# wq loaded in eight transfers of every eighth lane, the first ahead of w_out; x in two halves; w_out at a multiple of 512 bytes

## The chip, the cores and the metric

The kernel runs on one core of one Trainium2 chip. The metric is the time of one execution on the device, in microseconds (us); of several runs the median is given. The core's engines are named as in the profile: PE (TensorE), PEld (its weight loads), DVE (VectorE), ACT (ScalarE), POOL (GpSimd), SP (SyncE, which here only issues transfers). Transfers run on the core's 16 DMA engines. A *lane* is one of the 128 partitions of the on-chip memory.

## The reference

One decode step for four sequences: a layer norm of x, then attention over a cache of 4,096 keys and a gated MLP (gMLP) side by side, both added to x. All inputs are bfloat16.

```python
# x (4,1,640); k_cache, v_cache (4,32,4096,128); wq (640,4096); wo (4096,640)
# w_in (640,1728); w_sp (1,1); b_sp (1,); w_out (864,640)
xn = _layernorm(x)
q = (xn @ wq) as (4, 32 heads, 1, 128)
p = softmax(q . k_cache * 128**-0.5);  A = (p . v_cache) as (4,1,4096) @ wo
z = gelu(xn @ w_in);  z1, z2 = halves of z (864 each);  z2 = _layernorm(z2)
g = w_sp * z2 + b_sp;  B = (z1 * g) @ w_out
return x + A + B
```

The two caches are 134 MB each; wq is 5.2 MB, wo 5.2 MB, w_in 2.2 MB, w_out 1.1 MB.

## The kernel before

The attention is cut into NT = 16 tiles: eight heads (HT) of one sequence each. A tile of k or of v is 8.4 MB, [128 lanes, 256 rows of 128 numbers], and fills a slot of 64 KB in each lane: lane p holds 256 consecutive keys of one head. There are two slots for k (`k_slot`) and one for v (`v_slot`). The weights use the same slots before and after the caches: wq stands in a k slot at the start, w_in and w_out together in the v slot (`w_sb`), and wo in the v slot at the end. The last v tile goes to a k slot (`v_last`).

All large loads are issued by SP in the order of the program: w_out's first 768 rows (L109), wq (L114), w_in (L121), the other 96 rows of w_out in four transfers of four lanes each, lanes l, l+4, l+8, l+12 (L123), then k's tile 0 (L139). k's tile 1 follows when wq's slot is free, v's tile 0 (L145) when `w_sb` is, and from then on k and v alternate. ACT issues x (L104) and the two scalars w_sp and b_sp (L118, L119). Each issue carries a completion semaphore; there are eight of these for transfers, and they are used again and again.

wq has 640 rows of 4,096; lane p holds rows 5p to 5p+4, 40,960 bytes that are contiguous in both memories. w_in lies the same way (17,280 bytes a lane). w_out follows it in the lane, from byte 17,280: six rows of 1,280 bytes, 7,680 bytes a lane. x is four rows of 1,280 bytes in four lanes.

The work at the start: DVE makes the layer norm of x (L183 to L191), PE turns it (L203) into `xnT_r`, then q = xn wq is made in 40 matmuls (L271), turned into `qT` (L282), and `stage_q` spreads one sequence's q over the lanes (`qbc`, L435 and L443). `gmlp` follows on PE, DVE and ACT, reading w_in (L317) and at its end w_out (L216).

Then for each tile, in two halves: DVE multiplies the k tile by q in place (`product`, L449), adds its halves (`fold`, L463), PE sums by eights through an identity (`sums`, L475), DVE sums the rest (`row_sums`, L486); the maximum goes across the lanes (L495 to L524), ACT makes the exponentials (L542), DVE the mask by heads (L553), and PE the product with v (`weighted`, L568). After the last v tile, the output projection with wo (`group_proj`) ends the kernel. The order on PE, DVE, ACT and SP is the one written out in the loop; SP's loads wait where a slot is still being read.

Of the kernel before, what the change touches and what calls it, by code (L numbers as in the profile page):

```python
# [17 lines left out]
def kernel(  # L18
# [14 lines left out]
    nc = tc.nc  # L33
    P = nc.NUM_PARTITIONS
    Bsz, Sq, D = A_x.shape
    _, H, S, Dh = A_k_cache.shape
    HD = A_wq.shape[1]
    F = B_w_in.shape[1]
    Fh = F // 2
    DC = D // P  # L40
# [30 lines left out]
    NFC = NFF + TK  # L71
# [22 lines left out]
    def k_slot(name):  # L94
        return kp.tile([P, SLOT], BF16, tag="k", name=name)

    def v_slot(name):
        return vp.tile([P, SLOT], BF16, tag="v", name=name)
# [2 lines left out]
    start_t = pmp.tile([P, 4 * 512], BF16, tag="pm", name="start_t")  # L101
    x_bf = start_t[:Bsz, 0:D]
    xn_bf = start_t[:Bsz, D : 2 * D]
    nc.scalar.dma_start(out=x_bf, in_=A_x.flatten_outer_dims())  # L104

    w_sb = v_slot("w_sb")
    w_in_sb = w_sb[:, 0 : DC * F].rearrange("p (c n) -> p c n", c=DC)
    w_out_sb = w_sb[:, DC * F : DC * F + NFC * D].rearrange("p (k n) -> p k n", k=NFC)
    nc.sync.dma_start(  # L109
        out=w_out_sb[:, 0:NFF, :], in_=B_w_out[0 : NFF * P].rearrange("(p k) n -> p k n", k=NFF)  # L110
    )

    wq_t = k_slot("wq")[:, 0 : DC * HD].rearrange("p (c n) -> p c n", n=HD)
    nc.sync.dma_start(out=wq_t, in_=A_wq.rearrange("(p c) n -> p c n", c=DC))  # L114

    wsp_bf = const.tile([1, 1], BF16)
    bsp_bf = const.tile([1, 1], BF16)
# [4 lines left out]
    for l in range(TL // TE):  # L122
        nc.sync.dma_start(  # L123
            out=w_out_sb[:TL, NFF:NFC, :].rearrange("(e l) k n -> e l (k n)", e=TE)[:, l],
            in_=B_w_out[F0:Fh].rearrange("(e l k) n -> e l (k n)", e=TE, k=TK)[:, l],
# [56 lines left out]
    for i in range(NSTAT):  # L182
# [5 lines left out]
        out=rstd[:], in_=mv[:, 1:2], func=ACT.Sqrt, bias=eps_tile[:Bsz], scale=1.0  # L188
# [3 lines left out]
        out=xn_bf,  # L192
# [9 lines left out]
    for c in range(DC):  # L202
        nc.tensor.transpose(  # L203
            out=xnT_ps[:, c, :], in_=xn_v[:, c, :], identity=ident[:Bsz, :Bsz]
# [3 lines left out]
        out=xnT_r[:], in_=xnT_ps[:, :, :, None].to_broadcast([P, DC, Bsz, REP])  # L208
# [5 lines left out]
    def add_out(lhsT, rhs, start=False, stop=False):  # L214
# [14 lines left out]
        out=own[:], in_=ident_f[:].rearrange("p (h l) -> p h l", h=HT), axis=AX.X, op=ALU.add  # L229
# [4 lines left out]
        out=pick[:, :, GW - HT : GW],  # L234
        in_=ident_f[:].rearrange("p (j h c) -> p c h j", c=CB, h=HT),
# [5 lines left out]
        out=row_head_f[:],  # L241
        in_=ident_f[:WR, :WR].rearrange("p (g b h) -> p g h b", g=NG, h=HT),
# [5 lines left out]
        out=row_head[:],  # L248
        in_=row_head_f[:].rearrange("p g h -> p (g h)")[:, :, None].to_broadcast([WR, WH, WL]),
# [3 lines left out]
        out=row_batch_f[:],  # L253
        in_=ident_f[:WR, :WR].rearrange("p (g b h) -> p b g h", g=NG, h=HT),
# [12 lines left out]
    for t in range(2):  # L267
        for c in range(DC):
            for j in range(CG):
                n = CG * t + j  # L270
                nc.tensor.matmul(  # L271
                    out=q_ps[t][GW * j : GW * (j + 1), :],
# [6 lines left out]
    for t in range(2):  # L279
        qT_ps = ps_m.tile([P, HQ, CG, Bsz, REP], BF16, tag="m", name="qT_ps")  # L280
        for n in range(HQ):
            nc.tensor.transpose(  # L282
                out=qT_ps[:, n].rearrange("p j b r -> p (j b r)"),
                in_=q_rows[:, t, n * Dh : (n + 1) * Dh],
# [3 lines left out]
            out=qT[:, CG * HQ * t : CG * HQ * (t + 1), :].rearrange(  # L288
                "p (j n) b -> p n j b", n=HQ
            ),  # L290
            in_=qT_ps[:, :, :, :, 0],
# [382 lines left out]
    with tc.manual_schedule(engines={E.PE, E.DVE, E.Activation, E.SP}):  # L674
# [62 lines left out]
        for h, (_, queue) in enumerate(halves):  # L737
            cols = slice(D // 2 * h, D // 2 * (h + 1))
# [31 lines left out]
```

## Time and profile before

| | |
|---|---|
| median of 3 runs | 661.44 us (661.08 to 661.54) |
| the profiled execution: its time | 661.22 us |
| its span, first to last instruction | 659.4 us |
| mean granted TensorE clock | 0.713 |
| DVE busy | 492.3 us (75%) |
| PE busy, PEld busy | 298.0 us (45%), 129.0 us (20%) |
| ACT busy, POOL busy | 34.7 us (5%), 2.1 us (0%) |
| read from the chip's main memory | 282.24 MB, 428 GB/s over the span |

A row of the timeline gives the start in us from the span's start, the busy time in us, the engine, the line of the kernel, the operation, the tiles (out<-in) and how many were merged; in brackets stands the engine's idle time before it and what ended that. SPq and ACTq are the rows of the issuing queues: the time there is that of the issue, not of the transfer. A row by stretches gives from:to, then each engine's busy time with the number of instructions, the granted clock, the mean busy share of the 16 DMA engines, and GB/s. A row of waits gives the engine and line, what it waited for, the us in total, the number of times, and the longest.

### The profile page before, as it was taken

How to read it: one execution, taken by the hardware profiler on the slowest of the kernel's cores; microseconds unless marked ns; L12 is line 12 of the kernel's file. 1: busy time of each engine (PE TensorE's matmuls, PEld its weight loads, DVE VectorE, ACT ScalarE, POOL GpSimd, SP SyncE). 2: the span in 40 equal slices, each digit the busy share in tenths (PEclk: the TensorE clock that was granted, in tenths of full speed). 3: DMA queues.
4: the chain of work that ended last, by engine and by line, in shares of the span. 5: the costliest groups of instructions: out<-in, count | busy, mean ns of one | idle time of the engine just before them, and what ended most of it. 6: DMA issues, size and time to landing. Idle time of an engine off the chain costs nothing.

```text
span 659.4 us, 4721 instructions
## 1 busy us (share of the span) xinstructions
PE 298.0 (45%) x2099; PEld 129.0 (20%) x2099; DVE 492.3 (75%) x224; ACT 34.7 (5%) x95; POOL 2.1 (0%) x15
## 2 busy tenths in 40 slices
PE   0513464535426253542626344362734616273656
PEld 0301121212112021210202112120311202121223
DVE  1249999959597795959879569986959699695861
ACT  0300000000000000000000000000000000000000
POOL 1000000000000000000000000000000000000000
PEclk9756676876858687585868757786685758668698
DMA  9999999999999999999999999999999999999996
GB/s 378 445 441 445 406 442 438 426 445 426 429 441 430 429 442 426 441 426 421 445 437 434 441 422 425 445 430 437 434 430 433 446 417 434 429 445 438 437 399 296
DMA packets 5696, 282.55 MB, mean 429 GB/s; under 512 B 656, under 2 KB 796, under 8 KB 1068
## 3 DMA queue, kind: packets, MB, share of 16 engines
q1 hardware_dynamic: 5656, 282.24, 99.0%
q8 instruction: 16, 0.26, 0.1%
q14 instruction: 4, 0.03, 0.0%
q10 hardware_dynamic: 20, 0.01, 0.0%
HBM read 282.24 MB, written 0.01 MB: 428 GB/s over the span
## 4 chain that ended last, share of the span: by engine, by line
DMA 49%; DVE 40%; PE 8%; issue 2%; ACT 1%; SPq 0%; DVEq 0%
DMA k_nat<-in_A_k_cache_dram 42%; DVE k_nat L449 24%; DVE k_nat L463 12%; DMA v_last<-in_A_v_cache_dram 6%; PE s_ps L475 6%; DVE s_sb L486 3%; PE pv L568 1%; ACT p L542 1%; DMA w_sb<-in_B_w_out_dram 1%; DVE m L495 1%; PE mT L500 0%; DVE nm L505 0%; PE out_ps L216 0%; DVE wide L628 0%; PE o_ps L591 0%
## 5 line engine op out<-in xcount | busy, mean ns | idle before, releaser
L449 DVE TENSOR_TENSOR k_nat<-k_nat,qbc 128x16384 bf16<-128x16384 bf16 x32 | 278.0, 8688 | 96.3 <-DMA k_nat<-in_A_k_cache_dram 96.3
L475 PE MATMUL s_ps<-k_nat,ident 128*128 128x512 bf16 x528 | 186.7, 532 | 137.7 <-DVE k_nat L463 137.7
L463 DVE TENSOR_TENSOR k_nat<-k_nat 128x8192 bf16<-128x8192 bf16 x31 | 136.7, 4410 | 0.0
L475 PEld LDWEIGHTS <-ident 128*128 128x128 bf16 x528 | 65.9, 130 | 248.0 <-DVE k_nat L463 121.6
L500 PE MATMUL mT<-ident_f,m 128*1 128x128 f32 x16 | 5.9, 366 | 157.9 <-DVE m L495 157.9
L568 PE MATMUL pv<-v_nat,pm 128*32 128x512 bf16 x960 | 56.2, 388 | 0.8 <-DVE pm L553 0.8
L486 DVE TENSOR_REDUCE s_sb<-s_ps 128x128 f32<-128x1024 f32 x32 | 39.0, 1218 | 3.8 <-PE s_ps L475 3.7
L568 PEld LDWEIGHTS <-pm 128*32 128x32 bf16 x1024 | 27.5, 101 | 36.1 <-issue 10.8
L500 PEld LDWEIGHTS mT<-ident_f,m 128*1 128x1 f32 x16 | 1.3, 79 | 165.7 <-DVE m L495 154.5
L553 DVE TENSOR_TENSOR pm<-p,own_c 128x2048 bf16<-128x2048 bf16 x16 | 19.6, 1226 | 15.7 <-ACT p L542 15.7
L542 ACT ACTIVATE p<-s_sb,nb 128x256 bf16<-128x256 f32 x16 | 8.1, 508 | 388.5 <-DVE nb_h L524 388.5
L591 PE MATMUL o_ps<-e,pick 128*32 128x128 f32 x128 | 17.0, 276 | 11.2 <-ACT e L578 11.2
L591 PEld LDWEIGHTS o_ps<-e,pick 128*32 128x32 f32 x128 | 12.7, 109 | 18.7 <-ACT e L578 18.7
L578 ACT COPY e<-pv 128x512 f32<-128x512 f32 x16 | 9.4, 586 | 70.9 <-PE pv L568 61.3
L287 DVE COPY qT<-qT_ps 128x64 bf16<-128x64 bf16 x2 | 0.4, 224 | 15.5 <-PE qT_ps L282 15.5
L516 PE MATMUL nb_ps<-nm,ones_row 1*128 1x8 f32 x32 | 9.2, 359 | 6.0 <-DVE nm L505 6.0
L505 DVE TENSOR_REDUCE nm<-mT 1x8 f32<-1x128 f32 x16 | 4.5, 279 | 7.5 <-PE mT L500 7.5
L516 PEld LDWEIGHTS nb_ps<-nm,ones_row 1*128 1x128 f32 x32 | 7.7, 299 | 10.6 <-DVE nm L505 9.9
L271 PE MATMUL q_ps<-wq,xnT_r 128*32 128x512 bf16 x40 | 4.2, 603 | 11.2 <-DMA wq<-in_A_wq_dram 11.2
L443 ACT CAST qbc<-qbc_ps 128x128 bf16<-128x128 f32 x16 | 4.3, 267 | 94.6 <-PE qbc_ps L435 94.6
L568 PE MATMUL pv<-v_last,pm 128*32 128x512 bf16 x64 | 6.3, 577 | 4.1 <-DMA v_last<-in_A_v_cache_dram 4.1
L608 PE MATMUL den<-ones_col,acc_h 128*32 128x1 f32 x8 | 1.0, 194 | 15.5 <-DVE acc_h L601 15.5
(93 smaller groups left out, 72.6 us busy)
## 6 DMA issues: line engine op xcount, KB each, us to landing
wq<-in_A_wq_dram SPq DMA_DIRECT2D x1, 5120.0 KB, 16.3
wo<-in_A_wo_dram SPq DMA_DIRECT2D x1, 2560.0 KB
w_sb<-in_B_w_in_dram SPq DMA_DIRECT2D x1, 2160.0 KB, 21.0
wo<-in_A_wo_dram SPq DMA_DIRECT2D x1, 1760.0 KB
w_sb<-in_B_w_out_dram SPq DMA_DIRECT2D x1, 960.0 KB
wo<-in_A_wo_dram SPq DMA_DIRECT2D x1, 640.0 KB, 24.6
k_nat<-in_A_k_cache_dram SPq DMA_DIRECT2D x16, 39.2
v_nat<-in_A_v_cache_dram SPq DMA_DIRECT2D x15, 33.3
```

The costliest lines, as they stand in the source:

```text
L449: nc.vector.tensor_tensor(out=part(i, u), in0=part(i, u), in1=qbcs[i][:, None, :].to_broadcast([P, UC, Dh]), op=ALU.mult,)
L463: nc.vector.tensor_tensor(out=t[:, :, 0:HD2], in0=t[:, :, 0:HD2], in1=t[:, :, HD2:Dh], op=ALU.add)
L475: nc.tensor.matmul(out=sums_ps[i][:, c : c + SC], lhsT=ident[:], rhs=t[:, c : c + SC, g * RW : (g + 1) * RW], start=(g == 0), stop=(g == n ...
L486: nc.vector.tensor_reduce(out=scores[i][:, u * UC : (u + 1) * UC], in_=sums_ps[i][:], axis=AX.X, op=ALU.add,)
L495: nc.vector.tensor_reduce(out=m1[:], in_=scores[i][:], axis=AX.X, op=ALU.max)
L500: nc.tensor.transpose(out=mT[:], in_=maxes[i][:], identity=ident_f[:])
L516: nc.tensor.matmul(out=nb_ps[:], lhsT=ones_row[:], rhs=maxes[i][:], start=True, stop=True)
L542: nc.scalar.activation(out=probs[i][:], in_=scores.pop(i)[:], func=ACT.Exp, bias=maxes.pop(i)[:], scale=scale_qk, accum_out=accs[hg][:, b ...
L553: nc.vector.tensor_tensor(out=pm[:], in0=probs.pop(i)[:] .rearrange("p (n c) -> p n c", c=CB)[:, :, None, :] .to_broadcast([P, NB, HT, CB] ...
L568: nc.tensor.matmul(out=pvs[i][j * GW : (j + 1) * GW, :], lhsT=pm[:, n, :, :].rearrange("p h c -> p (h c)"), rhs=v_nat[:, n * CB : (n + 1) ...
L578: nc.scalar.copy(out=es[i][:], in_=pvs.pop(i)[:].rearrange("p (c d) -> p c d", d=Dh))
L591: nc.tensor.matmul(out=o_ps[hg // NG][own_rows(hg), :], lhsT=pick[:, c, GW - HT - HT * b : 2 * GW - HT - HT * b], rhs=e[:, c, :], start=(b ...
```

## The change

wq is loaded in eight transfers in place of one. Transfer l takes lanes l, l+8, l+16, ..., l+120: sixteen lanes of 40,960 bytes. The first is issued before w_out's load, the other seven after it. x is loaded in two transfers of 320 columns. w_out begins at byte 17,408 of the lane (the next multiple of 512 after w_in's 17,280).

```diff
-    nc.scalar.dma_start(out=x_bf, in_=A_x.flatten_outer_dims())
+    x_v = A_x.flatten_outer_dims()
+    for h in range(2):
+        cols = slice(D // 2 * h, D // 2 * (h + 1))
+        nc.scalar.dma_start(out=x_bf[:, cols], in_=x_v[:, cols])
 
     w_sb = v_slot("w_sb")
     w_in_sb = w_sb[:, 0 : DC * F].rearrange("p (c n) -> p c n", c=DC)
-    w_out_sb = w_sb[:, DC * F : DC * F + NFC * D].rearrange("p (k n) -> p k n", k=NFC)
+    w_at = -(-DC * F // 256) * 256
+    w_out_sb = w_sb[:, w_at : w_at + NFC * D].rearrange("p (k n) -> p k n", k=NFC)
+    wq_t = k_slot("wq")[:, 0 : DC * HD].rearrange("p (c n) -> p c n", n=HD)
+    QS = 8
+    wq_v = A_wq.rearrange("(e l c) n -> e l (c n)", l=QS, c=DC)
+
+    def load_wq(l):
+        nc.sync.dma_start(
+            out=wq_t.rearrange("(e l) c n -> e l (c n)", l=QS)[:, l], in_=wq_v[:, l]
+        )
+
+    load_wq(0)
     nc.sync.dma_start(
         out=w_out_sb[:, 0:NFF, :], in_=B_w_out[0 : NFF * P].rearrange("(p k) n -> p k n", k=NFF)
     )
 
-    wq_t = k_slot("wq")[:, 0 : DC * HD].rearrange("p (c n) -> p c n", n=HD)
-    nc.sync.dma_start(out=wq_t, in_=A_wq.rearrange("(p c) n -> p c n", c=DC))
+    for l in range(1, QS):
+        load_wq(l)
```

## The prediction

> **What bounds the kernel now.** I began with the page's row of DMA queues and the answer by stretches of the span, to see whether transfers or an engine set the pace.
>
> ```profile
> DMA packets 5696, 282.55 MB, mean 429 GB/s; under 512 B 656, under 2 KB 796, under 8 KB 1068
> q1 hardware_dynamic: 5656, 282.24, 99.0%
> ```
> ```profile
> core 0: us, PE busy (x) PEld busy (x) DVE busy (x) ACT busy (x) POOL busy (x), PEclk, DMA share, GB/s
> 23.00:43.00 20.00, 6.69 (x130) 5.78 (x130) 3.75 (x22) 3.91 (x8) 0.00 (x0) 0.55 1.01 435
> 43.00:120.00 77.00, 33.61 (x151) 13.22 (x152) 74.25 (x25) 3.98 (x10) 0.00 (x0) 0.63 1.00 433
> 120.00:600.00 480.00, 218.63 (x1406) 91.15 (x1405) 378.93 (x144) 20.64 (x63) 0.00 (x0) 0.71 1.00 434
> ```
>
> The sixteen DMA engines are occupied for 99.0% of the span by SP's queue alone (q1), and from 23 to 600 us their share is 1.00 at 433 to 435 GB/s. VectorE, the busiest engine, has 379 of 480 us in the long stretch. So the kernel lasts as long as its 282 MB take, plus the start before the engines move and the work behind the last load. A microsecond lost by the DMA engines at the start moves every later load by a microsecond; one won comes back whole as well.
>
> Then the start, in the timeline and in SP's own waits.
>
> ```profile
> 0.73 0.57 ACTq L104 DMA_DIRECT2D start_t<-in_A_x_dram  x1
> 0.73 0.40 SPq L109 DMA_DIRECT2D w_sb<-in_B_w_out_dram  x1
> 1.20 0.41 SPq L114 DMA_DIRECT2D wq<-in_A_wq_dram  x1
> ...
> 2.17 3.90 SPq L123 DMA_DIRECT2D w_sb<-in_B_w_out_dram  x4
> ...
> 6.12 16.05 SPq L139 DMA_DIRECT2D k_nat<-in_A_k_cache_dram  x2
> ...
> 17.58 4.21 PE L271 MATMUL q_ps<-wq,xnT_r 128*32 128x512 bf16 x40 [11.23 <-DMA wq<-in_A_wq_dram]
> ...
> 43.30 8.69 DVE L449 TENSOR_TENSOR k_nat<-k_nat,qbc 128x16384 bf16<-128x16384 bf16 x1 [9.75 <-DMA k_nat<-in_A_k_cache_dram]
> ```
> ```profile
> SPq L139 <- DMA wq<-in_A_wq_dram: 11.0, 1, 11.0
> SPq L123 <- DMA w_sb<-in_B_w_out_dram: 1.3, 1, 1.3
> ```
>
> TensorE waits 11.2 us for wq, VectorE 9.8 us for the first k tile: everything at the start waits for bytes in the order in which SP asked for them. The four issues at L123 take 3.9 us, since the last of them stood until w_out had landed (1.3 us): its completion semaphore is the one that w_out's load uses.
>
> The trace's packet records give the rates. One packet is one lane's row. A 65,536 B row of k takes an engine 2.418 us, wq's 40,960 B 1.514, w_in's 17,280 B 0.644, a 5,120 B row of wo 0.196. Two of these, (65,536 - 5,120) B in (2,418 - 196) ns, make 27.19 GB/s and 7.7 ns for each packet; the others fall on that line within 1 ns. Sixteen times 27.19 is 435: the ceiling seen above.
>
> **The change, part by part.** *wq in eight transfers.* The bytes stay (128 rows of 40,960 B, eight on each engine). Added are seven completion packets on each engine, 9 ns each in the records: 7 x 0.009 = 0.06 us. Also added are seven issues on SP, at 0.41 us (L114's row) to 0.73 (the longest at L123): 2.9 to 5.1 us. Queued behind them are w_in, the four tails of w_out, and k's first tile, whose issue goes from 6.1 to 9 or 11 us, and later if an issue must first see an older load land. What hides that is w_in: its eight packets occupy each engine for 8 x 0.644 = 5.15 us after wq is in. If each issue had to wait for the eighth load before it, k's would wait for about the last wq transfer, and would still come some 4 us before w_in is through. I cost it at nothing; without that cover it would be the 1.0 us from SP's first issue (0.73) to the first packet (1.75).
>
> *Which lanes a transfer writes.* This decides. Before, every large load goes to all 128 lanes at once. Afterwards a wq transfer goes to 16 lanes, l, l+8, ..., l+120, one on each engine. No row before shows that, so I bound it. At the lower end each engine keeps its 1.514 us for a packet: nothing. The near rows on that side are the tail loads of w_out: four lanes, four apart, on four engines, whose packets take 0.291 us, just as the 128-lane ones do; so lanes 4 to 12 apart do not disturb each other. x's four adjacent lanes, 1,280 B each, go in 0.053 us each though they overlap, but 5 KB may rest in a buffer. At the upper end the 27.2 GB/s belong to the way into a group of lanes, not to the engine. Large loads cannot tell the two apart, because all the lanes are written at once there. If two of the 16 lanes share a way, such as those 32 or 64 apart, a packet takes twice 1.514 us, and the eight in a row cost 8 x 1.514 = 12.1 us more. For packets of 40 KB I take the upper end: a ceiling so even, over four sizes and four tensors, looks like one fixed path, and 640 KB to 16 lanes is the first load that could ask a path for double. It is a judgement, and both ends stay in the range.
>
> [...]
>
> *The first transfer ahead of w_out.* In the records the engines' first packets start between 1.75 and 2.46 us and take 0.35 to 1.25 us instead of 0.291; an engine's eight packets of w_out end at 4.8 to 5.1, where 1.75 + 8 x 0.291 would be 4.1. So 0.7 to 1.1 us go in starting up. With 16 descriptors in front instead of 128 all the engines may start early and fill their pipes once, under a long packet; some of that delay is the first read itself and stays. I take -0.3 us, between 0 and -0.7. w_out lands later by one wq packet (1.5 to 3 us); it is read at 33.7 us, which is far off.
>
> *x in two halves.* One more issue on ACT, 0.57 us (L104's row), ahead of the two scalars and the square root. The layer norm would end near 7.1 instead of 6.5 us (xnT_r ends at 6.46); wq lands at 17. Nothing, with 10 us to cover it. Four packets more of some 0.03 us lie on four engines: 0.03.
>
> *w_out's place.* From byte 17,280 of a lane to 17,408. Its 7,680 B packets take 291 ns where the line gives 7.7 + 282.5 = 290: at most 1 ns for each of eight packets. Nothing.
>
> **The sum**, against the profiled execution's 661.22 us (0.22 below the median of the three): 661.22 + 12.1 + 0.06 + 0.03 - 0.3 = 673.1; against the median 673.3. I say 673.2. The 12.1 us meet no slack: k's tiles, v's and wo are all behind wq in the same queue, the DMA share stays 1.00 after 23 us, and VectorE's first product (43.3 us) waits for k's first tile already.
>
> **The rivals.** *No sharing*: the 27.2 GB/s are the engine's own. For it: the tail loads and x above show engines side by side undisturbed. Against: none of these has lanes 32 apart, and x is tiny. Then 661.22 + 0.09 - 0.3 = 661.0, between 660.6 and 661.5: not slower, and the sign of the forecast is lost. It decides as soon as a wq packet keeps 1.51 us. Were the whole start-up loss to go (1.1 us), it would be 660.2, still no faster than a measurement can tell; faster by more needs a gain for which I find no row.
>
> [...]
>
> *SP as the bound*: an issue waits for a landing and the engines run dry before k's first tile. It needs k's issue to come after w_in has ended, some 5 us later than worked out above; then 661.0 + 1 to 3 = 663. Against: SP is always ahead of the engines in the timeline, with k's first tile issued 16 us before its first packet.
>
> *More than two share* (lanes 32, 64 and 96 apart on one way): 3 x 12.1 = 36.3 more, 697. Nothing in the rows speaks for it more than for pairs.
>
> **How the numbers follow.** Pairs share: 0.61, alone 671.5 to 675 (the start-up term from 0 to -0.7, and some spread where wq meets w_out). Sharing unequal: 0.11. No sharing: 0.21. SP: 0.04. More than two: 0.03. The time is that of the likeliest, 673.2. Without the case of no sharing the range would leave out over 2 in 10, so it reaches from 660.8 to 675. What a measurement here can tell from no change is about 0.2%, 1.3 us. Slower: 0.61 + 0.11 + 0.03 + 0.03 = 0.78. Same: 0.18 of no sharing's 0.21 and the last 0.01 of SP's, 0.19. Faster: the 0.03 left, for a start-up gain that I can't price.
>
> **What the profile after would show.** Right: wq's packets at about 3.03 us where 1.514 stood; about 220 GB/s while wq loads, with a DMA share near 1; the first matmul at L271 near 29.5 instead of 17.58; the first product at L449 near 55 instead of 43.3; the same rates and idle times after that; v_last's landing later by the same 12 us. Packets of w_out and w_in, which go to all the lanes, would keep 0.29 and 0.64. Wrong: wq's packets still at 1.51, L271 within 1 us of 17.58, or a shift at L271 that is smaller at L449, which would mean that something after wq had slack.

## The result and the profile after

The changed kernel takes 675.41 us (median of 5 runs, 675.0 to 676.1) against 661.54 us (661.08 to 661.76): a ratio of 1.0212, 95% interval 1.0201 to 1.0224, or 13.9 us more. The profiled execution took 676.1 us, 0.7 above that median, with a span of 674.3 us.

The page after, with the two rows by 40 slices that show the start best (each slice is 16.9 us):

```profile
DMA  9999999999999999999999999999999999999996
GB/s 219 223 455 435 432 432 432 428 432 435 436 435 435 436 435 433 435 432 432 428 435 432 435 435 436 435 429 432 436 436 432 436 435 436 435 435 433 435 404 271
DMA packets 5816, 282.55 MB, mean 419 GB/s; under 512 B 772, under 2 KB 916, under 8 KB 1188
q1 hardware_dynamic: 5768, 282.24, 98.9%
```

The same two rows before (slices of 16.5 us):

```profile
DMA  9999999999999999999999999999999999999996
GB/s 378 445 441 445 406 442 438 426 445 426 429 441 430 429 442 426 441 426 421 445 437 434 441 422 425 445 430 437 434 430 433 446 417 434 429 445 438 437 399 296
```

The bytes are the same and the engines are just as occupied: the busy row cannot tell the two kernels apart. The GB/s row can. The first two slices move 219 and 223 GB/s, half of what the others do, where they moved 378 and 445 before; from the third on the rates are those of before, near 433. Here the engines were busy with their packets at half the rate, and only the GB/s row shows it.

By stretches of the span (engine times, clock, DMA share, GB/s), first a stretch before in which wq loads, then three after. A packet is counted whole where it starts, so in short stretches share and rate are rough and a share can pass 1:

```profile
5.00:17.00 12.00, 0.61 (x9) 0.48 (x10) 1.68 (x7) 0.03 (x1) 0.71 (x4) 1.00 0.93 404
```
```profile
17.00:29.00 12.00, 0.00 (x0) 0.00 (x0) 0.00 (x0) 0.00 (x0) 0.00 (x0) 1.00 1.01 208
43.00:120.00 77.00, 29.86 (x194) 12.85 (x195) 63.25 (x33) 5.40 (x13) 0.00 (x0) 0.63 1.01 435
120.00:600.00 480.00, 214.20 (x1336) 89.11 (x1335) 379.48 (x150) 20.58 (x64) 0.00 (x0) 0.70 1.00 434
```

From 17 to 29 us no engine computes and the DMA engines move 208 GB/s at a share of 1.01, where wq came at 404 GB/s before. After that the rates are those of before.

The timeline and SP's waits after (from w_in's issue on, the lines of the file are 14 further on than before):

```profile
0.73 0.64 SPq L118 DMA_DIRECT2D wq<-in_A_wq_dram  x1
...
2.04 7.73 SPq L118 DMA_DIRECT2D wq<-in_A_wq_dram  x7
...
6.91 0.48 DVE L197 BATCH_NORM_STATS2 stats<-start_t 4x6 f32<-4x320 bf16 x1 [4.27 <-DMA start_t<-in_A_x_dram]
...
10.39 0.33 DVE L221 COPY xnT_r<-xnT_ps 128x160 bf16<-128x160 bf16 x1 [0.45 <-PE xnT_ps L217]
...
26.45 11.05 SPq L153 DMA_DIRECT2D k_nat<-in_A_k_cache_dram  x2
...
33.42 3.70 PE L285 MATMUL q_ps<-wq,xnT_r 128*32 128x512 bf16 x40 [22.82 <-DMA wq<-in_A_wq_dram]
...
57.53 8.69 DVE L463 TENSOR_TENSOR k_nat<-k_nat,qbc 128x16384 bf16<-128x16384 bf16 x1 [9.84 <-DMA k_nat<-in_A_k_cache_dram]
```
```profile
SPq L137 <- DMA wq<-in_A_wq_dram: 9.7, 4, 2.6
SPq L118 <- DMA wq<-in_A_wq_dram: 3.4, 1, 3.4
```

TensorE's wait for wq goes from 11.2 to 22.8 us, and its first matmul from 17.58 to 33.42. VectorE's first product goes from 43.30 to 57.53, 14.2 us. The idle time before it is nearly the same (9.75 and 9.84), so nothing took the delay up. SP now stands for earlier landings 9.7 us at L137 and 3.4 at L118, since the eight completion semaphores go round; yet it asks for k's first tile at 26.45, while k's first packet starts only at 35.8, behind w_in. Those waits cost nothing.

The packet records say where the 14 us are. The columns wq, w_out, w_in and completion packets are one engine's share (the sum over all packets of a kind, divided by 16), in us:

| kernel | first packet starts (mean) | wq | w_out | w_in | completion packets | first k packet starts (mean) | time of the runs |
|---|---|---|---|---|---|---|---|
| before | 2.04 | 12.13 | 3.16 | 5.15 | 0.36 | 22.43 | 661.54 |
| after | 2.33 | 25.00 | 3.26 | 6.02 | 0.51 | 36.59 | 675.41 |
| after, run again with the experiments | 2.37 | 24.72 | 3.32 | 5.93 | 0.50 | 36.32 | 675.28 (before 661.09) |
| the split alone (an experiment below) | 2.04 | 24.75 | 3.14 | 5.61 | 0.50 | 35.52 | 674.00 (before 661.09) |

In the first two rows, 0.28 + 12.87 + 0.10 + 0.87 + 0.15 = 14.3 us, against 14.16 by which k's first packet comes later. A wq packet settles near 3.18 us; an engine's second packet (2.5 to 3.5 us) and its fifth (2.96 to 3.07 on nearly all engines) are shorter. The fifth takes about 3.0 us in every run below whose packets settle near 3.2 us, for a reason that no run shows. The mean is 3.126, and 1.517 before.

### The profile page after: what moved, and what is told of

It is laid out like the page before. It is cut to its first block, busy times and chain, and to the rows that moved or that the text cites. A ratio compares the mean times of both kernels' runs of the same rounds, so it can differ in the third digit from the quotient of the medians.

```text
span 674.3 us, 4734 instructions
## 1 busy us (share of the span) xinstructions
PE 296.2 (44%) x2099; PEld 128.4 (19%) x2099; DVE 492.4 (73%) x224; ACT 34.7 (5%) x95; POOL 2.1 (0%) x15
## 4 chain that ended last, share of the span: by engine, by line
DMA 54%; DVE 35%; PE 9%; issue 2%; ACT 1%; DVEq 0%; SPq 0%
DMA k_nat<-in_A_k_cache_dram 44%; DVE k_nat L463 21%; DVE k_nat L477 10%; PE s_ps L489 7%; DMA v_last<-in_A_v_cache_dram 6%; DMA wq<-in_A_wq_dram 4%; DVE s_sb L500 2%; PE pv L582 1%; ACT p L556 1%; DVE m L509 0%; PE mT L514 0%; DVE nm L519 0%; PE out_ps L230 0%; DVE wide L642 0%; PE o_ps L605 0%
## 5 line engine op out<-in xcount | busy, mean ns | idle before, releaser
L605 PE MATMUL o_ps<-e,pick 128*32 128x128 f32 x128 | 17.0, 276 | 11.2 <-ACT e L592 11.2
L285 PE MATMUL q_ps<-wq,xnT_r 128*32 128x512 bf16 x40 | 3.7, 542 | 22.8 <-DMA wq<-in_A_wq_dram 22.8
```

The costliest lines, as they stand in the source:

```text
L605: nc.tensor.matmul(out=o_ps[hg // NG][own_rows(hg), :], lhsT=pick[:, c, GW - HT - HT * b : 2 * GW - HT - HT * b], rhs=e[:, c, :], start=(b ...
```

## The experiments

The theory: groups of lanes have a common way in, some of the sixteen lanes of a transfer share one, and engines that stand on one way at the same time halve each other. The ways are my estimate: sixteen of 27.19 GB/s each would make the 435 GB/s of the loads to all lanes, and a shared one would explain the 3.13 us of wq's packets. How many there are, and which lanes share one, was supposed, and the runs test it. The rivals: eight transfers cost as such; reading rows that are 327,680 bytes apart in main memory costs; the other parts of the change cost.

**Eight transfers of all the lanes.** Only the shape of a transfer is changed.

```diff
-    wq_v = A_wq.rearrange("(e l c) n -> e l (c n)", l=QS, c=DC)
+    wq_v = A_wq.rearrange("(p c) n -> p (c n)", c=DC)
+    QW = DC * HD // QS
 ...
+        cols = slice(QW * l, QW * (l + 1))
 ...
-            out=wq_t.rearrange("(e l) c n -> e l (c n)", l=QS)[:, l], in_=wq_v[:, l]
+            out=wq_t.rearrange("p c n -> p (c n)")[:, cols], in_=wq_v[:, cols]
```

> wq still in eight transfers, the first ahead of w_out, x in halves, w_out at 17,408; but each transfer takes all 128 lanes and 5,120 bytes of each. Theory (shared ways into the lanes): no two engines meet, packets take 0.196 us as wo's do, 64 x 0.196 = 12.5 us on an engine instead of 12.1, plus 0.1 for completion packets and up to 0.3 at the start: 661.5 + 0.4 + 0.1 + 0.2 = 662.2 (661.3 to 662.8). Rival (eight transfers cost as such: more issues, waits for earlier landings, smaller transfers): stays near the changed kernel's 675.

Measured: 661.45 us, ratio 1.0005 (0.9996 to 1.0014). The timeline shows TensorE starting at 8.57 and then taking wq piece by piece:

```profile
8.57 1.49 PE L287 MATMUL q_ps<-wq,xnT_r 128*32 128x512 bf16 x10 [0.17 <-DVE xnT_r L223]
10.64 1.01 PE L287 MATMUL q_ps<-wq,xnT_r 128*32 128x512 bf16 x5 [0.57 <-DMA wq<-in_A_wq_dram]
```

So eight transfers, their issues and their waits cost nothing that can be measured, and q's matmuls may start 9 us earlier without any gain, because the queue of loads is what ends last.

**Sixteen neighbouring lanes.** Lanes 16l + e in place of l + 8e; the rows adjoin in main memory as well.

```diff
-    wq_v = A_wq.rearrange("(e l c) n -> e l (c n)", l=QS, c=DC)
+    wq_v = A_wq.rearrange("(l e c) n -> l e (c n)", l=QS, c=DC)
 ...
-            out=wq_t.rearrange("(e l) c n -> e l (c n)", l=QS)[:, l], in_=wq_v[:, l]
+            out=wq_t.rearrange("(l e) c n -> l e (c n)", l=QS)[l], in_=wq_v[l]
```

> As the changed kernel, but transfer l takes sixteen neighbouring lanes, 16l to 16l+15, whose rows are neighbours in main memory too. Theory (a way serves groups of four neighbouring lanes): four engines share each way, a 40 KB packet takes 4 x 1.59 = 6.4 us, 8 x 4.9 = 39 more than before, and about 2 more where wq meets w_in: 702 (697 to 706). Rival 1 (the cost lies in reading rows that are 327,680 bytes apart): the rows now adjoin, so near 661.5. Rival 2 (any transfer of sixteen lanes costs double): 675.

Measured: 694.75 us, ratio 1.051 (1.0494 to 1.0525). By stretches, and the timeline:

```profile
17.00:29.00 12.00, 0.00 (x0) 0.00 (x0) 0.00 (x0) 0.00 (x0) 0.00 (x0) 1.00 0.95 109
```
```profile
52.41 4.46 PE L285 MATMUL q_ps<-wq,xnT_r 128*32 128x512 bf16 x40 [39.48 <-DMA wq<-in_A_wq_dram]
```

Main memory is now read from adjoining rows and the rate falls to 109 GB/s, about a quarter. Rows far apart are not the cause, nor do sixteen lanes cost double whichever they are: both rivals fall. By the theory's count sixteen neighbours reach four ways. The size was below the expected range: packets settle at 5.65 us, not 6.4. If four engines stand on one way, they thus move 4 x 40,960 B in 5.654 us, 29.0 GB/s, while two move 2 x 40,960 B in 3.2 us, 25.6 GB/s. (The 109 GB/s above is two rounds of sixteen packets that start within 12 us; by the packets' durations it is 116.)

**Four apart, in one half of the lanes.** The edit is cut to the line that chooses the rows (lanes 64h + l + 4e); the destination changes likewise.

```diff
-    wq_v = A_wq.rearrange("(e l c) n -> e l (c n)", l=QS, c=DC)
+    wq_v = A_wq.rearrange("(h e l c) n -> h l e (c n)", h=2, l=QS // 2, c=DC)
 ...
```

> As the changed kernel, but a transfer takes sixteen lanes four apart in one half of the lanes: 64h + l + 4e. Theory A (lanes 32 apart share a way, lanes 64 apart don't): two engines on each of eight ways, packets near 3.19 us, 675 as the changed kernel. Theory B (lanes 64 apart share, lanes 32 apart don't; lanes eight apart over all 128 can't tell these apart): sixteen ways, packets 1.514 us, 662.

Measured: 674.27 us, ratio 1.0199 (1.0182 to 1.0216), packets near 3.17 us. Theory A stands: sixteen lanes of one half slow each other as those of the changed kernel do, so the sharing isn't between lanes 64 apart alone. That it is lanes 32 apart fits every run, but no run has such a pair by itself.

**Two apart.** The same number of engines on a way, on other lanes (32j + l + 2e); cut as above.

```diff
-    wq_v = A_wq.rearrange("(e l c) n -> e l (c n)", l=QS, c=DC)
+    wq_v = A_wq.rearrange("(j e l c) n -> j l e (c n)", j=4, l=2, c=DC)
 ...
```

> As the changed kernel, but a transfer takes sixteen lanes two apart, 32j + l + 2e: again eight ways and two engines on each, but the two lanes are in the same group of four neighbours, not 32 apart. Theory A (a way has one rate whatever the lanes, 25.7 GB/s as the pairs 32 apart show): packets 3.19 us, 674 to 675. Theory B (a way carries 29.0 GB/s, as the four neighbours of the sixteen adjacent lanes show, 4 x 40,960 B in 5.654 us, and loses 11% when its two lanes are 32 apart): packets 2 x 40,960 / 29.0 = 2.83 us, 8 x 0.36 = 2.9 us less than the changed kernel: 671 to 672.

Measured: 674.77 us, ratio 1.0207 (1.0193 to 1.0221), packets at 3.198 us. Theory A again: if two engines stand on one way, they get 2 x 40,960 B in 3.198 us, 25.6 GB/s, with lanes two apart, and hardly more in the changed kernel (25.8 at 3.18 us), whose pairs would be 32 apart. In these sets the supposed number of engines on a way fits the packets, and theory B's loss between distant lanes does not show. Why four get more than two in all stays open.

**Thirty-two lanes, every fourth.**

```diff
-    QS = 8
+    QS = 4
```

> As the changed kernel, but wq in four transfers of 32 lanes, every fourth lane: over a whole transfer all sixteen ways are reached, two lanes on each, and each engine has two rows. Theory A (what counts is which lanes are written at the same moment; engines take their rows in the order of the lanes, so at any moment they stand on eight ways, two on each): packets near 3.19 us, 674 to 675. Theory B (reaching all sixteen ways in one transfer is enough, as with 128 lanes, since rows go to the engine of their way): packets 1.51 us, 661.5. Between them, if engines drift so that half of them are on the other ways: 2.0 to 2.6 us, 666 to 671.

Measured: 661.85 us, ratio 1.001 (1.000 to 1.0019). Theory B, and my theory A falls: after their first packets the engines run wq at 1.514 us again. Even those first packets took 2.26 us on average, hardly more than the 2.17 of wq whole and first (below), which goes to all the lanes; in the changed kernel they took 3.11.

```profile
5.00:17.00 12.00, 0.61 (x9) 0.48 (x10) 2.35 (x9) 1.58 (x2) 0.71 (x4) 1.00 0.95 410
```
```profile
18.91 4.46 PE L285 MATMUL q_ps<-wq,xnT_r 128*32 128x512 bf16 x40 [8.48 <-DMA wq<-in_A_wq_dram]
```

At 410 GB/s nothing shows of engines that meet, though by the theory each way has two of the transfer's lanes. If the theory holds, both lanes of a way went to one engine, or the engines kept out of each other's way from the first packet on; the trace does not name a packet's engine, so which of the two is not settled. The remedy costs one character: with a step of four between the lanes the ratio is 1.001, where the changed kernel's is 1.0216.

Two things stay untested. No run takes sixteen lanes each of which, by the theory, has a way of its own. And in every run a lane takes the same rows of wq, so the lanes written and the places read in main memory never part. That the places are not the cause is argued: steps of 81,920, 163,840 and 327,680 bytes between the rows all gave packets of 3.17 to 3.20 us with sixteen lanes, and the step of 163,840 gave 1.514 with thirty-two.

**The other parts of the change.** Five kernels take it apart:

- the split alone: wq in eight transfers of every eighth lane, all behind w_out, x whole, w_out at 17,280;
- x in halves and w_out's place, wq in one transfer behind w_out;
- the same, with wq's one transfer ahead of w_out;
- the split with its first transfer ahead, x whole, w_out at 17,280;
- the split all behind w_out, x in halves, w_out at 17,408.

```diff
# the last of them, against the changed kernel
-    load_wq(0)
     nc.sync.dma_start(out=w_out_sb[:, 0:NFF, :], ...)
-    for l in range(1, QS):
+    for l in range(QS):
         load_wq(l)
```

> The kernel before with one edit: wq in eight transfers of every eighth lane, all behind w_out; x and w_out's place as before. Theory: the split is the whole cost, wq +12.9 us and +0.9 where its skew meets w_in, +0.1 completion packets: 675.3, and within 0.5 us of the changed kernel. Rival (part of the excess over 12.1 us comes from the first transfer ahead of w_out and from x in halves, whose packets started 0.3 us later and took up to 4.2 us): 1 us or more below the changed kernel, 674.4 or less.

Measured: 674.00 us, ratio 1.0196 (1.018 to 1.0211): the rival, if the changed kernel holds its time beside it.

> The changed kernel itself, on the chip of this call, to compare with: 1.0212 times before, 675.1. If it is near the 674.0 of the split alone, the rest of the change costs nothing.

Measured: 675.28 us, ratio 1.0216 (1.0202 to 1.023). It holds it: the split is 12.9 of the change's 14.2 us, and the rest brings 1.3.

> The kernel before with x in halves and w_out at 17,408, wq in one transfer behind w_out. Theory: both are nothing, 661.1 (660.8 to 661.5), with the layer norm later but far from wq's landing. Rival (the halves or the place carry part of the 2 us that the forecast lacked): 662 or more.

Measured: 661.13 us, ratio 1.0001 (0.9992 to 1.001): nothing, as forecast.

> As the changed kernel, but wq in one transfer of all 128 lanes, ahead of w_out; x in halves and w_out at 17,408 stay. Theory: packets 1.514 us again, no sharing; with long packets in front the start-up of 0.7 to 1.1 us that the kernel before shows is paid once under 40 KB: 661.1 + 0 to -0.7, so 660.7 (660.3 to 661.3). Rival (the start-up can't be had, since it is the first reads' own time, and x's second half lands late): 661.1 to 661.6.

Measured: 661.38 us, ratio 1.0006 (0.9997 to 1.0015). The rival: moving wq ahead wins nothing. An engine's first 40 KB packet takes 1.5 to 2.6 us instead of 1.514, on average 0.66 us over its time; w_out's first packets before were 0.47 over theirs.

> The split with its first transfer ahead of w_out, x whole and w_out at 17,280: the changed kernel without x in halves and without w_out's new place. The changed kernel stands 1.3 us above the split alone (675.3 against 674.0). Theory 1 (the first transfer ahead of w_out brings it: the first packets start 0.3 us later and under sharing, and leave the engines more out of step): 675.2, as the changed kernel. Theory 2 (x's second half, which now lands behind 40 KB packets, brings it): 674.0.

Measured: 675.26 us, ratio 1.0216 (1.02 to 1.0231).

> The split with all eight transfers behind w_out, x in halves and w_out at 17,408: the other half of the same pair. Theory 1 (the order brings the 1.3 us): 674.0, as the split alone. Theory 2 (x in halves brings it): 675.2.

Measured: 673.98 us, ratio 1.0195 (1.018 to 1.021). The two agree with theory 1: the 1.3 us come with the first transfer ahead of w_out, but only where that transfer is a split one, since whole it cost 0.3 us, within what can be told. x in halves and w_out's place are nothing in either setting. The last two rows of the table put 0.8 us of the 1.3 ahead of k's first packet: 0.33 in the later start, 0.32 in w_in, 0.18 in w_out. Where the rest lies is not shown.

None of these kernels beats the one before.

## Why the prediction was right and where it failed

- *What bounds the kernel*: right. The delay of k's first packet (14.16 us) went through to VectorE's first product (14.2) and to the end (14.9 between the two profiled executions, 13.9 between the medians), with no slack taken up. The forecast had named a shift that is smaller at the first product than at q's matmuls as a sign of slack, and it is smaller: 14.2 us against 15.8 (17.58 to 33.42). But TensorE waits for the last engine's wq packet, which ends 14.8 us later, and for its landing, which follows 0.7 us later than before; the loads behind wq do not wait for that engine: w_in's first packet starts at 29.36 us, while wq's last ends at 32.05.
- *Which lanes a transfer writes*: right in kind. The 128-lane pieces (661.45), the neighbours (694.75) and the every-fourth-lane form (661.85) leave the lanes of a transfer as the only cause tried that fits, with the two things untested that are named above. The choice of the upper end was a judgement, since no row before could tell the ends apart; the runs decide it only now. That a way carries 27.2 GB/s was my estimate from loads to all 128 lanes. No run shows it for a shared way: two engines moved 25.6 and four 29.0, if that many stood on one.
- *The size* is the step that failed: 11.9 us were forecast, 13.9 measured, above the 675 at which the range ended; VectorE's first product, forecast near 55 us, came at 57.53. Four terms of the sum were mis-sized, three here and the start in the next point. Twice 1.514 us, 3.03, was taken for a shared packet, which no run shows; 3.126 is measured on average: wq cost 12.9 us more in the profiled run, not 12.1. The transition from wq to w_in was put at nothing: w_in's packets were to keep 0.644 us, and the only spread that the forecast allowed for lay where wq meets w_out. They took 0.753 on average, so w_in took 6.02 us, not 5.15. Of these 0.87 us, 0.82 lie in packets that start before wq's last one ends. That engines which are done with wq write lanes of w_in while others still hold those ways for wq fits this; no run tests it alone. The completion packets cost 0.15, not 0.06, at up to 32 ns each instead of 9.
- *The first transfer ahead of w_out*: the term of -0.3 us had the wrong sign. SP's first issue takes 0.64 us for lanes with a step between them, against 0.40 for w_out's before and 0.385 for the sixteen neighbours, and the engines' first packets start 0.28 us later on average instead of earlier. The runs with and without this order differ by 1.3 us. The forecast took some of the start-up loss for the first read's own time and hoped to save the rest; wq whole and ahead of w_out (661.38) shows no gain, and what the loss consists of stays open.
- *x in two halves*: nothing, as said, but the layer norm did not end near 7.1 us. The second half's packets start at 4.60 to 5.90 us, each within 0.02 us of the end of an engine's first 40 KB packet, the second row of L197 starts at 6.91, and `xnT_r` ends at 10.7. The cover was large enough.
- *w_out's place*: nothing; with wq whole and first, every one of its packets at 17,408 takes 291 ns.
- *SP's queue*: SP did wait for landings, and w_in covered it, as worked out: k's first tile was asked for 9 us ahead of its first packet.
- *The rivals*: no sharing fell with the packets' 3.13 us. Unequal sharing, in which one engine of a pair draws ahead and then has the way to itself, fell too: that asks for packets of 1.514 us, and none of the changed kernel's wq packets took under 2.39. More than two engines on a way would fit neighbouring lanes (5.65 us a packet), not lanes eight apart.

## What to carry to other kernels

In these runs the speed of a transfer to a part of the lanes went with which lanes it wrote, however busy the DMA engines looked (410 GB/s at a share of 0.95 for every fourth lane, 208 at 1.01 for every eighth, 109 at 0.95 for sixteen neighbours): read GB/s beside the busy share. Cut a load along the columns and leave it on all 128 lanes, or step by four over all of them; both ran at the full rate here (420 and 410 GB/s, 661.45 and 661.85 us), where sixteen lanes two apart, four apart in one half or eight apart ran at half (packets of 3.13 to 3.20 us in place of 1.514), and sixteen neighbours at about a quarter (5.65 us). Where the loads' queue is the bound, price what the slow part leaves behind as well: the load behind wq took 17% longer here (w_in 6.02 us in place of 5.15).

## What the runs showed of the hardware that I had not expected

- If two engines stand on one way, they move 25.6 GB/s together (packets of 3.198 us), less than one alone (27.05 in wq's packets before, 1.514 us); four neighbours would move 29.0 (5.654 us).
- wq's landing follows its last packet later in the changed kernel. That packet ends at 17.23 us before, and its last completion is counted at 17.54; in the changed kernel it ends at 32.05, and the completion is counted at 33.07: 1.0 us instead of 0.3 in which TensorE still waits.
- As the first transfer, an issue for lanes with a step cost SP more: 0.58 us for 32 lanes four apart and 0.62 to 0.64 for sixteen, against 0.385 to 0.41 for 16 or 128 neighbouring lanes.
